# A GFNet-and-MLP kernel: the first transforms take turns over four PSUM banks, and one split store at the end changes its queue

## The chip, the cores and the metric

The kernel runs on one core of a Trainium2 chip. The metric is the time of one execution in microseconds (us), the median over several runs. Five engines work side by side: PE (TensorE, matrix products), DVE (VectorE), ACT (ScalarE), POOL (GpSimd) and SP (SyncE, which here only issues DMAs). PE writes its results to PSUM banks; DVE or ACT must copy a bank out before PE may fill it again.

## The reference, cut to what matters

```python
def _attn_ref(x, filt_r, filt_i):              # x: (8, 3008, 256)
    X = np.fft.rfft(x, axis=1)
    F = (filt_r + 1j * filt_i)[None, :, :]     # (1505, 256)
    y = np.fft.irfft(X * F, n=x.shape[1], axis=1)
    return y.astype(np.float32)

def _moe_ref(x, w_in, w_out):                  # x: (24064, 256), d_ff = 2048
    h = x @ w_in
    g = np.maximum(0.01 * h, h)
    return (g @ w_out).astype(np.float32)
```

The result is `_moe_ref` of the filtered sequence: a Fourier transform along 3008 tokens, a product with a filter, the inverse transform, and two matrix layers with a leaky ReLU between them.

## The kernel before, in words

**Transforms.** 3008 is factored as 94 x 32. A batch's transform has four stages, each a row of small matmuls into one PSUM bank that ACT or DVE copies out: `s1_group` (L254, copied at L257), `s2_group` (L303, multiplied by the filter on DVE at L309 to L315 and added on POOL at L318), `sa_group` (L325, L327) and `sb_group` (L346, copied into `yt` at L336). Between stages the data is turned through DRAM by DMAs that SP issues. The first batch takes a way of its own, without DRAM, written out by hand in the list `FIRST`; its last six groups are called later, by `late_sb` (L446, matmuls at L437).

**The two layers.** The 24064 tokens form 47 chunks of 512. `moe1` (L495) makes the first layer: for each pair of 128-column blocks four matmuls (L505) into a double bank `ph`, of which there are two in turn, and one leaky ReLU on ACT (L510) from `ph` into `gt`. One chunk later the second layer follows: `plain` (L626, matmuls at L630) for the first three chunks, then `products`, a Strassen-Winograd form of it with seven half-size products (L561 to L624, matmuls at L569), whose sums are made on DVE (L542, L594, L602 and others).

**Banks.** PSUM's eight banks are the two double banks `ph0` and `ph1`, three single banks `pf0` to `pf2`, and `po_ps`. The opening uses the first seven, and `po_ps` for matmuls on zeros (`keep_warm`). Then `single.pop()` (L489) takes `pf2` out of the list from which `bank("pf", ...)` (L154) deals to the transforms in turn; `pf2` (as `psp_last`) and `po_ps` become `out_banks`, the second layer's. So from there on the transforms alternate between `pf0` and `pf1`.

**Order.** Every step is a function put at a planned time with `at(time, f)` in a heap; at the end the heap is emptied in order of time, and each function issues its instructions, on whichever engine, in that order. A planned time is in units in which a chunk lasts `SL = 8`: `moe1` of chunk 0 has times 0 to 7.5, and the second layer of chunk 0 begins at 8.01. The transforms' groups of batches 1 to 7 are placed by `plan` and the loop after it (L688 to L706), at least `GAP = 0.6` units apart. Engines run their queues strictly in this order, so an instruction that waits holds up those behind it on its engine.

**Stores.** A chunk's output leaves in four stores of 128 tokens, `tj = 2 * i + j`, two from each of the tiles `rows(ci, 0)` (h0) and `rows(ci, 1)` (h1). Output tokens lie in groups of `QT = 376`, so a store that meets such a border becomes two DMAs (the loop in `store`, L548). In the last chunk, number 46, one border falls 8 tokens into store `tj = 1` (i = 0, j = 1), which is then one DMA of 8 tokens (2 x 4 rows of 256) and one of 120 (30 x 4 rows). For chunk 46 the stores with j = 1 are issued by ACT, those with j = 0 by SP; for all other chunks all are issued by SP. h1 is stored when its last DVE sum (L602) is done, h0 when the very last sum of the kernel (L594) is done.

Of the kernel before, what the change touches and what calls it, by code (L numbers as in the profile page):

```python
# [75 lines left out]
def kernel(  # L76
# [9 lines left out]
    nc = tc.nc  # L86
# [7 lines left out]
    NCHUNK = TOK // CH  # L94
    assert NCHUNK * CH == TOK
    SL = 8
# [52 lines left out]
    single = [psp.tile([P, CH], FP32, name=f"pf{i}") for i in range(3)]  # L149
    po_ps = psp.tile([P, 2, D], FP32, name="po_ps")  # L150
    psp_last = single[-1]
# [12 lines left out]
    def at(time, f):  # L164
        clock["n"] += 1
        heapq.heappush(work, (time, clock["n"], f))
# [315 lines left out]
    for step in FIRST.split(","):  # L482
# [7 lines left out]
    out_banks = [t[:].rearrange("p (a t d) -> p a t d", a=2, t=2)  # L490
                 for t in (psp_last, po_ps.rearrange("p a d -> p (a d)"))]

    gts, osts, phs = {}, {}, {}

    def moe1(ci, ct):  # L495
# [52 lines left out]
    def store(ci, tj, of, queue=nc.sync):  # L548

        t, end = ci * CH + tj * P, ci * CH + (tj + 1) * P  # L550
        lo = 0
        while t < end:
            e = min(end, (t // QT + 1) * QT)
            b, h = divmod(t // QT, N2 // 4)
            row = b * N + (t % QT) // 4 * N2 + 4 * h
            queue.dma_start(
                bass.AP(tensor=out.tensor, offset=out.offset + row * D,
                        ap=[[N2 * D, (e - t) // 4], [D, 4], [1, D]]), of[lo : lo + e - t])
            lo, t = lo + e - t, e
# [15 lines left out]
    def rows(ci, i):  # L575

        if (ci, i) not in osts:
            osts[ci, i] = outp.tile([P, 2, 3, P], FP32, tag="ost", name=f"ost_c{ci}_h{i}")
        return osts[ci, i]

    def stores(ci, i, of=range(2)):
        for j in of:
            store(ci, 2 * i + j, rows(ci, i)[:, j, 0:2, :].rearrange("p k d -> p (k d)"),
                  nc.scalar if ci == NCHUNK - 1 and j else nc.sync)

    def twice(po):
        ap = [list(v) for v in po.ap]
# [4 lines left out]
    def last_product(ci):  # L592
        def after(po):
            add(rows(ci, 0)[:, :, 1], po, rows(ci, 1)[:, :, 2], AL.add)  # L594
            soon(AFTER[5], lambda: stores(ci, 0))
        return product(ci, lambda: sum_places(ci)[3], b22, after, 3)

    def products(ci):
        a11, a12, a21, a22 = (lambda i=i, j=j: quarter(ci, i, j) for i in range(2) for j in range(2))

        def after5(po):
            add(rows(ci, 1)[:, :, 1:3], twice(po), part[1], AL.add)  # L602
            soon(AFTER[5], lambda: stores(ci, 1))

        def m1():
            return product(ci, a11, b11, lambda po: nc.scalar.copy(t1, po))

        def m2():
            return product(ci, a12, b21, lambda po: add(rows(ci, 0)[:, :, 0], po, t1, AL.add))

        def m7():
            return product(ci, lambda: sum_places(ci)[1], wt[2], lambda po: add(v7, po, t1, AL.add), 1)

        if ci == NCHUNK - 1:
            items = last_product(ci - 1) + m1() + m7() + m2()
        elif ci > W0:
            items = m1() + last_product(ci - 1) + m2() + m7()
        else:
            done["products"] += 1
            items = m1() + [lambda: None] * (2 * NCH) + m2() + m7()  # L620
        items += product(ci, lambda: sum_places(ci)[2], wt[1], lambda po: add(part[1], twice(po), part[0], AL.add), 2)
        items += product(ci, a22, wt[3], lambda po: add(rows(ci, 1)[:, :, 0], po, u3, AL.add))
        items += product(ci, lambda: sum_places(ci)[0], wt[0], after5, 0)
        return items + last_product(ci) if ci == NCHUNK - 1 else items  # L624
# [44 lines left out]
    for b in range(1, B):  # L669
        z = 47 * (b - 4) if b > 4 else 0  # L670
        p = PLANS[min(b, 4) - 1]
# [82 lines left out]
```

## Time and profile before

| What | Value |
|---|---|
| median of 6 runs | 749.81 us (749.54 to 752.38) |
| the profiled execution's own time | 751.97 us |
| its span, first to last instruction | 750.2 us |
| PE busy | 738.1 us (98%) |
| ACT busy | 559.2 us (75%) |
| DVE busy | 501.4 us (67%) |
| POOL busy | 169.5 us (23%) |
| granted TensorE clock | 0.999 |
| last matmul begins, last sum on DVE begins | 744.2, 744.51 us |

The span is counted from the first instruction; 1.8 us of the execution lie around it. PE's busy time counts pipelined matmuls with modelled ends, so a PE that is busy is not thereby at its fastest; how fast it goes is read from the distance between the starts of its matmuls. The first batch's opening ends at about 35 us, the chunks of the two layers with the transforms between them fill the time to about 744 us, and the last 6 us hold only the stores and the closing barrier.

### The profile page before, as it was taken

The numbers are of one execution on the slowest core, as the hardware profiler recorded it, in microseconds if no ns is written. First come the engines' busy times: TensorE is split into PE (matmuls) and PEld (weight loads), VectorE is DVE, ScalarE is ACT, GpSimd is POOL, SyncE is SP. The second block draws the span as 40 slices with busy tenths as digits, with TensorE's granted clock in tenths as the row PEclk, the third lists the DMA queues.
The fourth block names the chain that finished last, engine by engine and source line by source line (L and its number), as shares of the span: only waits on it lengthen the run. The fifth ranks groups of instructions, "written<-read, shape, count | busy, mean of one in ns | idle before, by whom it ended". The sixth has DMA issues, their size and how long they took to land.

```text
span 750.2 us, 19408 instructions
## 1 busy us (share of the span) xinstructions
PE 738.1 (98%) x8017; PEld 528.8 (70%) x8017; DVE 501.4 (67%) x684; ACT 559.2 (75%) x755; POOL 169.5 (23%) x171
## 2 busy tenths in 40 slices
PE   8999999999999999999999999999999999999996
PEld 3656667677677777877778777777777777777775
DVE  5986646776666776766667757766676676565565
ACT  3776797888778778787787787787777777777662
POOL 5603421432232212221232232121212210000000
PEclk9999999999999999999999999999999999999999
DMA  9997798887866567655675656544454333111011
GB/s 206 227 222 187 187 219 222 208 202 194 203 181 168 143 192 184 153 140 163 197 177 156 158 152 173 157 138 112 142 161 120 100 107 107 50 54 54 32 53 59
DMA packets 119560, 113.64 MB, mean 151 GB/s; under 512 B 16352, under 2 KB 92768, under 8 KB 119280
## 3 DMA queue, kind: packets, MB, share of 16 engines
q1 hardware_dynamic: 104127, 94.66, 42.5%
q0 software_dynamic: 15056, 17.49, 15.8%
q8 instruction: 62, 1.02, 0.6%
q10 hardware_dynamic: 289, 0.26, 0.1%
q14 instruction: 26, 0.21, 0.1%
HBM read 57.51 MB, written 50.33 MB: 144 GB/s over the span
## 4 chain that ended last, share of the span: by engine, by line
PE 94%; DVE 2%; DMA 2%; ACT 1%; POOL 0%; issue 0%; SPq 0%; DVEq 0%; POOLq 0%
PE ph L505 43%; PE po_ps L569 18%; PE pf L569 18%; PE pf L254 3%; PE pf L346 3%; PE pf L325 2%; PE pf L303 2%; PE pf L630 1%; PE po_ps L630 1%; DMA p_b_g<-p_b_g 1%; DMA big<-in_x_dram 1%; PE po_ps L368 1%; POOL y_b_g L318 0%; ACT yt L336 0%; PE ph L396 0%
## 5 line engine op out<-in xcount | busy, mean ns | idle before, releaser
L510 ACT ACTIVATE gt_c<-ph 128x1024 f16<-128x1024 f32 x376 | 385.3, 1025 | 134.9 <-PE ph L505 124.2
L505 PE MATMUL ph<-yt,w_in_sb 128*128 128x512 f16 (+7 forms) x1728 | 447.3, 351 | 0.2 <-ACT yt L336 0.2
L569 PEld LDWEIGHTS <-gt_c 128*128 128x128 f16 x2800 | 202.3, 98 | 91.3 <-issue 0.2
L318 POOL TENSOR_TENSOR y_b_g<-p_b_g,p_b_g 128x512 f16<-128x512 f32 x84 | 119.8, 1427 | 414.3 <-DMA p_b_g<-p_b_g 241.3
L569 PEld LDWEIGHTS <-big 128*128 128x128 f16 x2128 | 151.3, 98 | 62.9 <-issue 1.4
L505 PEld LDWEIGHTS <-w_in_sb 128*128 128x128 f16 x1728 | 137.4, 98 | 20.3 <-issue 0.7
L312 DVE TENSOR_TENSOR p_b_g<-pf,fb_sb 128x512 f32<-128x512 f32 x78 | 53.7, 688 | 32.4 <-PE pf L303 17.1
L569 PE MATMUL po_ps<-wt_sb,gt_c 128*128 128x128 f16 x704 | 70.0, 219 | 0.0
L569 PE MATMUL pf<-wt_sb,gt_c 128*128 128x128 f16 x688 | 68.4, 219 | 0.0
L569 PE MATMUL pf<-w_out_sb,gt_c 128*128 128x128 f16 x720 | 67.9, 219 | 0.0
L569 PE MATMUL po_ps<-wt_sb,big 128*128 128x128 f16 x720 | 67.4, 219 | 0.1
L569 PE MATMUL pf<-wt_sb,big 128*128 128x128 f16 x704 | 67.2, 219 | 0.0
L257 ACT CAST big<-pf 128x512 f16<-128x512 f32 x100 | 58.3, 588 | 11.9 <-PE pf L254 10.5
L569 PE MATMUL po_ps<-w_out_sb,gt_c 128*128 128x128 f16 x688 | 66.0, 219 | 0.0
L336 ACT CAST yt<-pf 128x376 f16<-128x376 f32 x120 | 56.4, 473 | 10.8 <-PE pf L346 7.7
L542 DVE TENSOR_TENSOR big<-gt_c 128x2048 f16<-128x2048 f16 (+1 forms) x46 | 57.4, 1248 | 0.1
L315 DVE TENSOR_TENSOR p_b_g<-pf,fa_sb 128x512 f32<-128x512 f32 x84 | 57.2, 681 | 0.2
L542 DVE TENSOR_TENSOR gt_c<-gt_c 128x2048 f16<-128x2048 f16 x43 | 55.5, 1290 | 1.0
L542 DVE TENSOR_TENSOR big<-big,gt_c 128x2048 f16<-128x2048 f16 (+1 forms) x45 | 55.6, 1236 | 0.1
L542 DVE TENSOR_TENSOR big<-gt_c,big 128x2048 f16<-128x2048 f16 (+1 forms) x45 | 54.5, 1211 | 0.0
L327 ACT CAST big<-pf 128x512 f16<-128x512 f32 x84 | 49.0, 584 | 6.1 <-PE pf L325 4.2
L254 PE MATMUL pf<-x_sb,small_sb 94*128 94x512 f16 x112 | 42.7, 381 | 0.6 <-ACT big L257 0.6
(88 smaller groups left out, 620.3 us busy)
## 6 DMA issues: line engine op xcount, KB each, us to landing
dz<-big SPq DMA_DIRECT2D x98, 256.0 KB
p_b_g<-p_b_g SPq DMA_DIRECT2D x156, 128.0 KB
out_dram<-ost_c_h SPq DMA_DIRECT2D x119, 128.0 KB
big<-dz SPq DMA_DIRECT2D x42, 256.0 KB
big<-dz SPq DMA_DIRECT2D x56, 192.0 KB
x_sb<-in_x_dram POOLq DMA_DIRECT2D x40, 192.0 KB, 4.3
x_sb<-in_x_dram POOLq DMA_DIRECT2D x2, 768.0 KB, 8.4
w_in_sb<-in_moe_w_in_dram POOLq DMA_DIRECT2D x1, 1024.0 KB, 12.5
```

Source lines behind the costliest of these rows:

```text
L254: nc.tensor.matmul(ps, fwd1[:N1], x_sb[:N1, ds(2 * g, 2), :], start=True, stop=True)
L257: copy(st[:, ds(2 * (g % 2), 2), :], ps)
L312: nc.vector.tensor_tensor(p2[:], ps, fb, AL.mult)
L315: nc.vector.tensor_tensor(p1[:], ps, fa, AL.mult)
L318: ("y", b, g), lambda: nc.gpsimd.tensor_tensor(y1[:], p1[:], p3[:], AL.add)))
L327: nc.scalar.copy(st2[h % 4][:, ds(2 * (g % 2), 2), :], ps)
L336: copy(yv, ps.rearrange("p c a -> p a c"))
L346: nc.tensor.matmul(ps[:, j, :], z2[h % 4][:K4, j, ts(dt, P)], i1_sb[:K4, 4 * h + j, :], start=True, stop=True)
L505: nc.tensor.matmul(ph[:, j, ds(t - ci * CH, e - t)], w_in_sb[:, dt, ts(ct, P)], yt[:, dt, ds(t % N, e - t)], start=(dt == 0), stop=(dt == ...
L510: nc.scalar.activation(gts[ci][:, ds(2 * g, 2), :], ph, AF.Lrelu)
L542: nc.vector.tensor_tensor(*(v[:, ds(c0, n)] for v in (o, i0, i1)), op)
L569: nc.tensor.matmul(po[:, t], a()[:, c, ts(t, P)], w[:, c, :], start=(c == 0), stop=(c == NCH - 1))
```

## The change

Two edits.

The first puts `pf2` and `po_ps` back into the list from which the transforms' banks are dealt, and takes them out again at planned time 7.6, shortly before the second layer's first matmul. In that stretch the transforms take turns over four banks, not two. Fourteen groups fall into it: thirteen of `s1_group` of batch 1 and one `late_sb`. The counter of turns runs on, and fourteen is even, so every group after it gets the bank that it had before.

The second changes the queue of two of the last chunk's four stores: ACT issues those with i = j (h0 j 0 and h1 j 1), SP those with i != j. The store that the border splits (h0 j 1, two DMAs) goes from ACT to SP, and h0 j 0 (one DMA) from SP to ACT.

```diff
     out_banks = [t[:].rearrange("p (a t d) -> p a t d", a=2, t=2)
                  for t in (psp_last, po_ps.rearrange("p a d -> p (a d)"))]
 
+
+    single += [psp_last, po_ps.rearrange("p a d -> p (a d)")]
+    at(SL - 0.4, lambda: single.__delitem__(slice(2, 4)))
+
     gts, osts, phs = {}, {}, {}
...
     def stores(ci, i, of=range(2)):
         for j in of:
             store(ci, 2 * i + j, rows(ci, i)[:, j, 0:2, :].rearrange("p k d -> p (k d)"),
-                  nc.scalar if ci == NCHUNK - 1 and j else nc.sync)
+                  nc.scalar if ci == NCHUNK - 1 and i == j else nc.sync)
```

The lines after the first edit stand four lines lower in the changed kernel.

## The prediction

> **What bounds the kernel now.** I read the page's busy rows first, then PE's waits, then the two places that the diff touches: the stretch of planned times 0 to 7.6, and the end.
>
> ```profile
> PE 738.1 (98%) x8017; PEld 528.8 (70%) x8017; DVE 501.4 (67%) x684; ACT 559.2 (75%) x755; POOL 169.5 (23%) x171
> ```
>
> PE is busy in 98% of the span, and its granted clock (0.999 on average) leaves nothing to win. Time can come only from PE's gaps, or from what lies after its last matmul. The longest waits of PE after its very first one, in the whole trace (line, what it waited for: total us, times, longest):
>
> ```profile
> PE ph L374 <- ACT x_sb L459: 1.1, 1, 1.1
> PE pf L325 <- POOL y_b_g L318: 1.1, 1, 1.1
> PE pf L303 <- DVE p_b_g L315: 1.0, 1, 1.0
> PE pf L254 <- ACT big L257: 0.6, 1, 0.6
> ```
>
> Only the last row can belong to the first edit: one matmul of an s1 group waited until ACT had copied an earlier group out of the same bank. Its place, in PE's timeline (start, us, instruction, idle before) and ACT's:
>
> ```profile
> 41.06 0.38 PE L254 MATMUL pf<-x_sb,small_sb 94*128 94x512 f16 x1
> 41.27 0.59 PE L505 MATMUL ph<-yt,w_in_sb 128*128 128x512 f16 x2
> 41.80 0.45 PE L437 MATMUL pf<-i_sb,big 128*64 128x94 f16 x8
> 42.81 0.38 PE L254 MATMUL pf<-x_sb,small_sb 94*128 94x512 f16 x1 [0.56 <-ACT big L257]
> ```
>
> ```profile
> 41.26 1.02 ACT L510 ACTIVATE gt_c<-ph 128x1024 f16<-128x1024 f32 x1 [0.36 <-PE ph L505]
> 42.17 0.58 ACT L257 CAST big<-pf 128x512 f16<-128x512 f32 x1
> 42.64 0.49 ACT L336 CAST yt<-pf 128x376 f16<-128x376 f32 x1
> 43.65 2.11 ACT L510 ACTIVATE gt_c<-ph 128x1024 f16<-128x1024 f32 x2 [0.52 <-PE ph L505]
> ```
>
> The group of 41.06 is copied out only at 42.17 to 42.75, behind a leaky ReLU on ACT. The second group after it (42.81) has the same bank, and PE, in order, stands still. Elsewhere in this stretch PE goes on without a gap: an s1 matmul and two of the first layer start every 0.65 us, three of 512 columns at 0.22 each.
>
> The end, from the timeline of the two issuing queues, and SP's waits:
>
> ```profile
> 744.33 0.54 SPq L556 DMA_DIRECT2D out_dram<-ost_c_h  x1
> 744.97 0.55 SPq L556 DMA_DIRECT2D out_dram<-ost_c_h  x1
> ...
> 744.34 0.68 ACTq L556 DMA_DIRECT2D out_dram<-ost_c_h  x1
> 745.11 1.21 ACTq L556 DMA_DIRECT2D out_dram<-ost_c_h  x1
> 746.37 0.93 ACTq L556 DMA_DIRECT2D out_dram<-ost_c_h  x1
> ...
> SPq L749 <- DMA out_dram<-ost_c_h: 3.3, 3, 1.7
> ```
>
> SP has issued its two stores by 745.52. ACT needs until 747.30: its first, then the piece of 8 tokens (1.21), then the piece of 120 (0.93). SP's longest last wait, 1.7 us, is for that piece to land, at about 749.0; the closing barrier takes the rest to 750.2. So the end is set by ACT's queue.
>
> **The change part by part.** *Four banks.* The instructions and their order on PE, DVE, ACT and POOL stay as they were but for bank names and waits; nothing is added. The group of 42.81 gets a bank whose copy (on DVE) was over by 41.51, so it may start when PE gets there. The same switch from L437 to a full-width matmul at 48.00 took 0.37 us start to start (48.00 to 48.37); so 41.80 + 0.37 = 42.17 in place of 42.81: 0.63 us.
>
> What is late next? ACT's next leaky ReLU began at 43.65, 0.42 after the last first-layer matmul that it needs. With PE 0.63 earlier these are ready at 43.02, and ACT is free of its two copies at 43.13: it starts at about 43.05 and ends at 44.07. PE writes that `ph` bank again with the first-layer matmul now at 44.76, then at 44.13. Margin 0.06. I take no new stall; at worst a tenth or two comes back. A new wait for the other `ph` bank stands at 42.81 (was 43.45), and the ReLU that frees it ended at 42.28.
>
> The borrowed banks are the second layer's. Its first matmul (L630, `po_ps`, 46.49, then 45.86) gets a wait for DVE to have copied the last s1 group out of `po_ps`; that group's matmul is the one at 44.54, copied by about 45.6, then 0.6 earlier: 0.8 before it is needed. Behind that wait all of PE would queue. Its wait for the weights `w_out_sb` moves to the weight load; their DMA was issued at 29.2 and took 14.1, so they are there at 43.3. `pf2` is wanted at 51.1, long after. On DVE the copies follow PE; L664, filling 41.43 to 42.37, is done before the earlier group is ready at 42.58. If that cover failed, DVE's 0.95 would put the copy behind, not PE.
>
> Does 0.63 reach the end? From 46 us on the turning stores, loads, exchanges and copies all start from PE's results and SP's order, so they shift with PE. The DMA engines are busy near fully from 37 to 52 us, and the last s1 store is issued at 51.74, when this is nearly over; the loads at 56.67 wait in SP's queue for the store of the second output (DVE L635 at 55.47), PE's work again. PE's later stalls (1.0 at 66, 1.1 at 213) hang on DVE and on POOL, whose inputs shift likewise. I carry 0.63.
>
> *The split store.* SP now issues h1 j 0 (744.33 to 744.87), the 8-token piece, the 120-token piece; ACT h1 j 1 and h0 j 0. On SP the same two shapes stand in this trace at 261.90 and 408.47:
>
> ```profile
> 261.90 0.73 SPq L556 DMA_DIRECT2D out_dram<-ost_c_h  x1
> ...
> 408.47 0.93 SPq L556 DMA_DIRECT2D out_dram<-ost_c_h  x1
> ```
>
> By these rows: 744.97 + 0.73 + 0.05 + 0.93 = 746.68 against 747.30: 0.62 us gained. ACT's h0 j 0, 745.11 + 0.6 to 0.7, is done by 745.8 and lands before.
>
> [...] the 8-token piece took 1.21 on ACT beside SP's 0.55, 0.48 above its 0.73 on SP alone; yet ACT's first store, begun with SP's, took 0.68 and not 0.54 + 0.54. [...] Between 0.1 and 0.62 I take 0.45: [...] of the two contended rows one shows 0.14 lost and one 0.48.
>
> *Sum.* 0.63 + 0.45 = 1.08. The profiled execution, 751.97 with its span of 750.2, would be 750.9 with a span of 749.1. It stood 2.2 above the median of the runs; off that median, 749.81, the sum gives 748.7.
>
> **Rivals.** *PE's stall moves to ACT.* ACT follows so closely that the 0.06 margin fails, and the leaky ReLU is PE's next wait. For it: ACT goes 43.65 to 45.76 without a pause. Against: in the stretch it still has idle time, 0.52 before 43.65. If it takes 0.4 of the 0.63[...]: 749.81 - 0.23 - 0.1 = 749.5, no measurable change.
>
> *A later wait goes as well.* PE's two long later stalls, 1.0 on DVE at 66 us and 1.1 on POOL at 213 us, end when a chain of DVE work, exchange DMA and POOL add ends. The exchanges make POOL wait 241 us in all, 11.7 at the longest, so their length varies with what they meet. If the shift lets one such chain through, 0.5 to 1.1 is added: 749.81 - 1.08 - 0.7 = 748.0. Against: each shifts with PE, so only chance meetings decide.
>
> *Slower: the exchange comes late.* The same chain in the other direction, at L325 in batches 1 to 7: PE asks for `y` 0.63 earlier, while the exchange meets other traffic and does not come earlier. One such slip exists and costs 1.1. With three more, 3.3 - 1.08: 752.0. It decides from about 2.6 us of new waits on. Against: the exchange is issued from DVE products that follow PE.
>
> **How the numbers follow.** 0.2% of 749.81 is 1.5 us, about what a measurement of this kernel can tell from no change; five of the six runs lie within 749.5 to 750.4. Both parts as summed (0.7 to 1.3): 0.60; the gain of 1.1 is only 0.4 from the bound, and with that scatter a quarter of it, 0.15, reads as over 1.5. A later wait goes as well: 0.28. Stall moved to ACT: 0.05. Late exchange: 0.07. Faster 0.15 + 0.28 = 0.43, same 0.45 + 0.05 = 0.50, slower 0.07. The range, 747.9 to 749.7, holds the sum with both ends of the tail (748.6 and 749.1), most of the case with a later wait, and scatter at both ends; the late exchange and the extremes are left out.
>
> **What would show it.** In the changed profile: PE's wait at L254 for ACT is gone and the s1 matmul after the first L437 row starts 0.37 after it; the second layer's first matmul comes about 0.63 earlier, the last matmul too; SP's last issue ends about 1.8 after its 8-token piece began, with ACT done before. Wrong would be: a new wait of PE on ACT L510 near 44 us, a larger wait at L325, or SP's last issue ending no earlier, counted from the last sum, than ACT's did, 2.4 after it.

## The result, and the profile after

The changed kernel takes 748.94 us in the median (748.11 to 750.21, 20 runs), beside 750.10 for the kernel before in the same runs (41). The ratio is 0.9982, 95% interval 0.9976 to 0.9988: 1.2 us by the medians, 1.35 by the ratio (0.0018 x 750.1); the interval runs from 0.9 to 1.8 us, so the gain is clear of noise. The forecast was 748.7, 1.1 below the median that it started from.

PE's waits after the change (the whole table of that view):

```profile
PE po_ps L368 <- DVE one L226: 1.2, 1, 1.2
PE pf L303 <- DVE p_b_g L315: 1.0, 1, 1.0
PE ph L392 <- issue: 0.5, 1, 0.5
PE ph L420 <- POOL prod L400: 0.4, 1, 0.4
PE ph L437 <- DVE big L429: 0.2, 1, 0.2
PE ph L374 <- ACT x_sb L459: 0.2, 1, 0.2
```

The row of L254 waiting for ACT is gone. So is the row of L325 waiting for POOL, 1.1 us, which no part of the change aimed at; more on it below. PE's timeline at the place of the old wait:

```profile
40.62 0.38 PE L254 MATMUL po_ps<-x_sb,small_sb 94*128 94x512 f16 x1
40.84 0.59 PE L509 MATMUL ph<-yt,w_in_sb 128*128 128x512 f16 x2
41.36 0.45 PE L437 MATMUL pf<-i_sb,big 128*64 128x94 f16 x8
41.74 0.39 PE L254 MATMUL pf<-x_sb,small_sb 94*128 94x512 f16 x1
...
43.70 0.38 PE L509 MATMUL ph<-yt,w_in_sb 128*128 128x512 f16 x1
```

and ACT's beside it:

```profile
41.74 0.58 ACT L257 CAST big<-po_ps 128x512 f16<-128x512 f32 x1
42.20 0.49 ACT L336 CAST yt<-pf 128x376 f16<-128x376 f32 x1
42.60 2.11 ACT L514 ACTIVATE gt_c<-ph 128x1024 f16<-128x1024 f32 x2
```

The group of 40.62 now writes `po_ps`. ACT copies it as late as before, at 41.74, but the group that starts at the same 41.74 has another bank and does not wait: 0.38 us from L437's start to L254's, before 1.01 (41.80 to 42.81). ACT's next leaky ReLU starts at 42.60 without a pause; the first of its pair ends at about 43.62, and PE fills that `ph` bank again at 43.70. PE did not catch up with it.

The end, on SP and then on ACT:

```profile
741.82 0.54 SPq L560 DMA_DIRECT2D out_dram<-ost_c_h  x1
...
742.45 0.70 SPq L560 DMA_DIRECT2D out_dram<-ost_c_h  x1
...
743.20 0.90 SPq L560 DMA_DIRECT2D out_dram<-ost_c_h  x1
```

```profile
741.82 0.67 ACTq L560 DMA_DIRECT2D out_dram<-ost_c_h  x1
...
742.59 0.70 ACTq L560 DMA_DIRECT2D out_dram<-ost_c_h  x1
```

The last sum on DVE starts at 741.99. SP's pieces of 8 and 120 tokens take 0.70 and 0.90; its last issue ends at 744.10, 2.1 after that start. Before, ACT's ended at 747.30, 2.8 after 744.51. So the last issue ends 0.7 earlier, counted from the sum.

**Where the profiled 3.3 us went.** The two profiled spans, 750.2 and 746.9, differ by more than the medians do. Three marks of each timeline split the difference: the first matmul of the first layer (L505, now L509), the first of the second layer (L630, now L634), and the start of the last sum on DVE (L594, now L598).

| stretch | before | after | difference |
|---|---|---|---|
| start to first layer | 34.96 | 34.46 | -0.50 |
| first layer to second layer | 11.53 | 10.98 | -0.55 |
| second layer to last sum | 698.02 | 696.55 | -1.47 |
| last sum to end of span | 5.65 | 4.95 | -0.70 |

Only the second and the fourth row contain what was changed, 1.25 us together. The first and the third vary from one execution to the next, as the experiments show.

### The profile page after: what moved, and what is told of

Read it like the earlier page. It is cut to its first block, busy times and chain, and to the rows that moved or that the text cites. A ratio compares the mean times of both kernels' runs of the same rounds, so it can differ in the third digit from the quotient of the medians.

```text
span 746.9 us, 19408 instructions
## 1 busy us (share of the span) xinstructions
PE 737.9 (99%) x8017; PEld 528.7 (71%) x8017; DVE 503.6 (67%) x684; ACT 559.2 (75%) x755; POOL 167.0 (22%) x171
## 4 chain that ended last, share of the span: by engine, by line
PE 91%; DMA 5%; DVE 1%; POOL 1%; ACT 1%; SPq 1%; issue 0%; POOLq 0%; DVEq 0%
PE ph L509 42%; PE po_ps L573 18%; PE pf L573 18%; PE pf L254 3%; PE pf L346 3%; PE pf L325 2%; PE pf L303 2%; PE pf L634 1%; PE po_ps L634 1%; DMA f_sb<-fwd_const 1%; DMA fa_sb<-in_filt_i_dram 1%; DMA out_dram<-ost_c_h 1%; DMA dz<-big 1%; POOL prod L400 0%; DVE big L546 0%
## 5 line engine op out<-in xcount | busy, mean ns | idle before, releaser
L509 PE MATMUL ph<-yt,w_in_sb 128*128 128x512 f16 (+7 forms) x1728 | 447.3, 351 | 0.2
L318 POOL TENSOR_TENSOR y_b_g<-p_b_g,p_b_g 128x512 f16<-128x512 f32 x84 | 117.2, 1397 | 415.1 <-DMA p_b_g<-p_b_g 240.0
L509 PEld LDWEIGHTS <-w_in_sb 128*128 128x128 f16 x1728 | 137.5, 98 | 19.7 <-DVE yt L336 0.4
L546 DVE TENSOR_TENSOR gt_c<-gt_c 128x2048 f16<-128x2048 f16 x43 | 57.8, 1345 | 1.0
L254 PE MATMUL pf<-x_sb,small_sb 94*128 94x512 f16 x109 | 41.6, 381 | 0.0
```

Source lines behind the costliest of these rows:

```text
L254: nc.tensor.matmul(ps, fwd1[:N1], x_sb[:N1, ds(2 * g, 2), :], start=True, stop=True)
L318: ("y", b, g), lambda: nc.gpsimd.tensor_tensor(y1[:], p1[:], p3[:], AL.add)))
L509: nc.tensor.matmul(ph[:, j, ds(t - ci * CH, e - t)], w_in_sb[:, dt, ts(ct, P)], yt[:, dt, ds(t % N, e - t)], start=(dt == 0), stop=(dt == ...
L546: nc.vector.tensor_tensor(*(v[:, ds(c0, n)] for v in (o, i0, i1)), op)
```

## The experiments

The theory: the change takes away one wait of PE (0.6 us) and shortens the issuing of the last stores (0.5 to 0.7); these add, and nothing else changed. Rivals: PE's earlier start removes the wait at L325 as well; the issues of SP and ACT lengthen each other, as ACT's row of 1.21 us beside SP's 0.55 suggested, and that eats up the gain at the end; the two edits need each other.

**The banks alone.** The changed kernel with the stores of before:

```diff
-                  nc.scalar if ci == NCHUNK - 1 and i == j else nc.sync)
+                  nc.scalar if ci == NCHUNK - 1 and j else nc.sync)
```

> The four banks alone, stores as before. Theory: PE's wait of 0.6 us at L254 is gone and nothing else changes, so the median falls by 0.6 us (0.5 to 0.7) and PE's stream from 46 us on runs 0.6 earlier; the tail from the last DVE sum's start to the end stays at 5.65 us. Rival (the wait of PE at L325 for POOL near 213 us goes because PE runs earlier): the fall is 1.9 us, in every run. Rival (the two edits need each other): no fall.

Measured: 749.55 against 750.13, ratio 0.9995 (0.9986 to 1.0003). The medians say -0.58, what was expected, though the interval alone cannot tell it from nothing. The profile can: the wait is gone, the stretch from the first to the second layer is 10.92 us and not 11.53, and the tail is 5.6. A fall of 1.9 lies outside the interval (its far end is 1.05): the wait at L325 is not part of the edit's effect.

**The stores alone.** The kernel before with the diff's second edit only.

> The queue swap alone, banks as before. Theory: PE's stream is that of before, with the 0.6 us wait at L254; the tail from the last DVE sum's start to the end falls from 5.65 to 4.9 us, and the median by 0.7 us (0.6 to 0.8). Rival [...]: the tail falls by 0.1 to 0.3 only. Rival (the gain is all in PE's part): no fall.

Measured: 749.57 against 750.13, ratio 0.9992 (0.9984 to 1.0001), -0.56 by the medians; again the interval alone does not exclude no change. Of its PE waits, the one in question:

```profile
PE pf L254 <- ACT big L257: 0.6, 1, 0.6
```

The wait at L254 is back, the stretch from the first to the second layer is 11.53 again, and the tail is 4.95, not the rival's 5.35 to 5.55. In the profiles each edit does its own part without the other, so neither needs the other. The medians fit a plain sum (0.58 and 0.56 alone, 1.16 together), but with such intervals that is weak support. The wait at L325 is missing here too, with two banks in turn.

**Three banks.** Only `pf2` is lent, stores as before:

```diff
-    single += [psp_last, po_ps.rearrange("p a d -> p (a d)")]
-    at(SL - 0.4, lambda: single.__delitem__(slice(2, 4)))
+    single += [psp_last]
+    at(SL - 0.4, lambda: single.__delitem__(slice(2, 3)))
```

> Three banks in the early stretch in place of four (pf2 added, po_ps not), stores as before. Theory: one more bank is enough, since the group that waited then takes the bank of the third group before it, which DVE had emptied 1.2 us earlier; the same fall as with four banks, 0.6 us (0.5 to 0.7). Rival (four are needed, since copies on DVE run late too): a wait of PE at L254 stays, and the fall is under 0.3 us.

Measured: 749.53 against 750.13, ratio 0.9991 (0.9983 to 0.9999). PE's timeline:

```profile
41.01 0.45 PE L437 MATMUL pf<-i_sb,big 128*64 128x94 f16 x8
41.39 0.39 PE L254 MATMUL pf<-x_sb,small_sb 94*128 94x512 f16 x1
```

The same 0.38 from start to start, and the stretch is 10.92. One more bank was enough; the fourth took nothing more off this stretch.

**The pieces apart.** Four banks, and the split store's two pieces on two queues:

```diff
-            queue.dma_start(
+            (queue[lo > 0] if isinstance(queue, tuple) else queue).dma_start(
...
-                  nc.scalar if ci == NCHUNK - 1 and i == j else nc.sync)
+                  (nc.sync, nc.scalar) if ci == NCHUNK - 1 and (i, j) == (0, 1)
+                  else nc.scalar if ci == NCHUNK - 1 and i and j else nc.sync)
```

> Four banks, and the two pieces of the split store on two queues: SP issues h1 j 0, h0 j 0 and the 8-token piece, ACT issues h1 j 1 and the 120-token piece. Theory (issue times simply add on each queue): SP ends 0.55 + 0.05 + 0.70 = 1.3 us after it may begin, ACT 0.1 + 0.95; the last issue ends 0.3 to 0.35 us earlier than in the changed kernel, whose SP needs 1.65, and the median is 0.3 us below it, 1.6 below before. Rival [...]: the three issues add up to about 2.2 us whatever the queue, no gain over the changed kernel or a loss of up to 0.5.

Measured: 748.54 against 750.13, ratio 0.9979 (0.9971 to 0.9986); tail 4.57. On ACT:

```profile
742.82 0.69 ACTq L560 DMA_DIRECT2D out_dram<-ost_c_h  x1
...
743.62 1.44 ACTq L560 DMA_DIRECT2D out_dram<-ost_c_h  x1
```

The piece of 120 tokens took 1.44 us on ACT, where it had taken 0.93 as ACT's last DMA before and 0.90 on SP after. Neither expectation has that number: not the plain sum, and not issues in turn, which ACT's 0.70 beside SP's 0.70 in the changed kernel (742.59 to 743.29 and 742.45 to 743.15) contradicts. ACT's last issue thus ended 2.06 us after the last sum's start, hardly earlier than SP's 2.11 in the changed kernel, and yet the tail is 0.38 shorter; the reason comes further down. What ACT's slow pieces have in common, here and in the kernel before, is another thing: each was the first DMA of ACT that was not of the full 32 x 4 shape.

**All of h0 on ACT.** The kernel before with SP silent beside ACT's pieces:

```diff
-                  nc.scalar if ci == NCHUNK - 1 and j else nc.sync)
+                  nc.scalar if ci == NCHUNK - 1 and (j or i == 0) else nc.sync)
```

> Banks as before; all of h0's last stores on ACT (h1 j 1, h0 j 0, the 8-token piece, the 120-token piece), SP issues only h1 j 0. No SP issue lies beside ACT's pieces. Theory A (the 8-token piece took 1.21 us on ACT because SP was issuing beside it[...]): it now takes 0.73. Theory B (ACT is slow the first time that it issues a DMA whose outer count is not a multiple of 16): it takes about 1.2 again and the 120-token piece behind it 0.93. Either way the last issue ends later than before.

Measured (one run, 750.55 us, of which only the profile is read), ACT's last three issues of four:

```profile
743.00 0.69 ACTq L556 DMA_DIRECT2D out_dram<-ost_c_h  x1
743.73 1.21 ACTq L556 DMA_DIRECT2D out_dram<-ost_c_h  x1
744.99 0.95 ACTq L556 DMA_DIRECT2D out_dram<-ost_c_h  x1
```

With nothing beside it, the 8-token piece takes 1.21 again. Theory A (contention with SP) falls; theory B (the first of its kind on ACT) stands, though its bound at multiples of 16 was not shown: no run put a 16 x 4 store on ACT. A full store takes ACT 0.69 here with SP silent, as long as beside SP. The tail grew to 6.4 us.

**A first DMA of that kind earlier.** Two kernels made from the pieces apart. In one, which ran once (748.85 us), ACT also issues the split store of chunk 43:

```diff
-                  else nc.scalar if ci == NCHUNK - 1 and i and j else nc.sync)
+                  else nc.scalar if (ci == NCHUNK - 1 and i and j) or (ci, i, j) == (43, 0, 1) else nc.sync)
```

> The kernel of e4_pieces_apart, plus: the split store of chunk 43 (two DMAs, 40 and 88 tokens) issued by ACT and not SP, some 40 us before the end; it holds ACT up there, so only the tail is to be read. Theory B, with or without forgetting over 700 us: ACT's first of those two is slow (1.2 or more), the second about 0.85, and the 120-token piece at the end takes 0.93. Theory A: it takes 1.44 at the end.

```profile
713.27 1.40 ACTq L560 DMA_DIRECT2D out_dram<-ost_c_h  x1
...
714.72 0.84 ACTq L560 DMA_DIRECT2D out_dram<-ost_c_h  x1
...
743.00 0.89 ACTq L560 DMA_DIRECT2D out_dram<-ost_c_h  x1
```

The first, of 40 tokens, is now the slow one; the one at the end takes 0.89, beside SP's issues as in the pieces apart. The tail is 4.60, no shorter than the pieces apart have it. In the other, ACT issues a DMA of 2 rows of 8 bytes in the opening:

```diff
     nc.scalar.activation(one[:], one[:], AF.Lrelu)
+    warm_q = cpool.tile([2, 4], FP16, name="warm_q")
+    nc.scalar.dma_start(warm_q[:], small_d.ap()[0:2, 0, 0:4])
```

> The kernel of e4_pieces_apart, plus one tiny DMA (2 rows of 8 bytes) that ACT issues in its idle opening, before the first x has landed; the rest is the same. Theory B (first issue of that kind on ACT is slow[...]): ACT's 120-token piece at the end takes 0.93 us and not 1.44, the last issue ends about 0.3 us earlier than in e4, and the median is 0.3 below e4's, 1.9 below before. Theory A [...]: the piece still takes 1.44, no change to e4. Theory B with forgetting [...]: as A.

```profile
742.49 0.97 ACTq L562 DMA_DIRECT2D out_dram<-ost_c_h  x1
```

0.97 in place of 1.44, after 741 us in between. But the tail only fell from 4.57 to 4.50, where I had expected 0.3. The DMA engines tell more. A row of this view begins with its window in us and ends with their busy share and their GB/s; between stand the five engines' busy times, all zero by then, and the clock. First the pieces apart, then the kernel with the early DMA:

```profile
744.00:745.20 1.20, 0.00 (x0) 0.00 (x0) 0.00 (x0) 0.00 (x0) 0.00 (x0) 1.00 0.92 324
745.20:746.00 0.80, 0.00 (x0) 0.00 (x0) 0.00 (x0) 0.00 (x0) 0.00 (x0) 1.00 0.63 170
...
742.90:744.10 1.20, 0.00 (x0) 0.00 (x0) 0.00 (x0) 0.00 (x0) 0.00 (x0) 1.00 0.95 324
744.10:744.80 0.70, 0.00 (x0) 0.00 (x0) 0.00 (x0) 0.00 (x0) 0.00 (x0) 1.00 0.70 192
```

Counted from the last sum's start, the engines move the last stores from 1.0 to 3.0 us in the one and from 1.0 to 2.9 in the other, without a pause, though ACT's last issue ends at 2.06 in the one and at 1.59 in the other. (In the changed kernel they end at 3.4: there the 120-token piece is SP's third issue, and begins only at 1.20.) ACT's own packets end between 2.9 and 3.0 in every profile of the pieces apart, with a row of 1.44, 0.97 or 0.89. So the long row did not hold up its own transfer, and ACT's issuing no longer set this end. Whether the transfers did, or SP's third issue, which ends at 1.76 in all of them, no run here separates. In the kernel before it was otherwise. There the 120-token piece had to wait on ACT's queue behind the long row, and the DMA engines stood still for a whole microsecond (the end of that piece's issue is 747.30):

```profile
746.90:747.90 1.00, 0.00 (x0) 0.00 (x0) 0.00 (x0) 0.00 (x0) 0.00 (x0) 1.00 0.00 0
```

The median of the kernel with the early DMA, 747.97 against 750.32, ratio 0.9964 (0.9952 to 0.9976), fell by more than the tail explains; only six runs stand behind it.

**Once more, together.** The changed kernel and the two best, on one chip.

> The changed kernel, unchanged, beside the next two on one chip. Expected 1.2 to 1.4 us below before (0.61 from the banks, 0.71 from the stores); tail from the last sum's start to the end 4.95 us.

> The kernel of e4_pieces_apart again. Its tail was 4.57 us, so 0.38 below the changed kernel if the tail is all that differs.

> The kernel of e9_act_split_early again. Its tail was 4.50 us: ACT's piece had become 0.46 us faster, but SP, whose three issues end 1.76 us after the sum's start in both, then set the end. If the tail is all that differs, it lies 0.07 us below e11, no difference that can be measured; if the extra DMA of the opening shortens the opening, it lies 0.3 us or more below.

| kernel | median | before | ratio (95%) | tail |
|---|---|---|---|---|
| changed kernel | 748.73 | 750.28 | 0.9980 (0.9972 to 0.9988) | 4.94 |
| pieces apart | 748.75 | 750.28 | 0.9980 (0.9974 to 0.9987) | 4.53 |
| pieces apart, early DMA on ACT | 748.38 | 750.28 | 0.9977 (0.9968 to 0.9987) | 4.50 |

The changed kernel's 1.55 by the medians is above the 1.2 to 1.4 expected. The shorter tail of the pieces apart shows in every profile, but its 0.4 us does not show in these medians, nor is the early DMA's 0.37 clear of the intervals. All three beat the kernel before; which of them is best stays open. Whether the early DMA does something to the opening was not settled: its two profiles have the first layer begin at 34.11 and 34.09, those of the pieces apart at 35.55 and 34.31.

**The kernel before, profiled again.**

> The kernel before, unchanged, for a second profile. Theory (the 1.3 us stall of PE at L325 near 213 us is a chance meeting of transfers and no property of this kernel): it is absent or of another size; the 0.6 us wait at L254 near 42 us and the tail of 5.65 us are there again. Rival (it belongs to the two-bank order): it is there again with 1.0 to 1.3.

From its PE waits:

```profile
PE ph L374 <- ACT x_sb L459: 1.9, 1, 1.9
...
PE pf L254 <- ACT big L257: 0.6, 1, 0.6
```

The wait at L254 and the tail of 5.65 are there again; the wait of 1.1 at L325 is not, nor is it in the two other profiles with two banks in turn. The opening's wait for x, 1.1 in the first profile, is 1.9. Over the thirteen profiles of this study the first layer begins anywhere from 33.85 to 35.55 us, and the stretch from the second layer to the last sum lasts 696.5 to 698.0, under both bank orders: the changed kernel's own second profile has 697.8. So the first and third row of the table above are scatter, and the two rows that the edits touch explain 1.25 us, with which the 1.35 of the ratio agrees.

## Why the prediction was right

*The bound.* PE sets the pace (busy in 98% of the span before, 99% after), and time came only from one gap of PE and from behind its last matmul, as argued.

*Four banks: 0.63.* The stretch is 11.53 in all four profiles with two banks in turn, 10.92 in eight of the nine with more, and 10.98 in the changed kernel's first: 0.61, and 0.58 by the medians. No new stall: the margin to ACT's ReLU, put at 0.06, was about 0.08. That the gain reached the end rests on the medians and on the long stretch behind, which was no longer with the banks lent (696.5 to 697.8) than without (696.7 to 698.0).

*The split store: 0.45.* The direction was right and this term was sized too small: 0.70 in the profiles (5.65 to 4.95). The rows of the trace, 0.73 and 0.93, gave 0.62; the rest lies in SP's pieces, which took 0.70 and 0.90. The 0.17 that I had cut off was an estimate for queues that issue in turn, and the weak step. Its lower end, a gain of 0.1, puts SP's 0.73, ACT's 0.55 and SP's 0.93 one behind the other from 744.97 on, to 747.2, which is 2.7 after the sum's start; the changed kernel took 2.1, with SP's and ACT's issues side by side at 0.70 and 0.70. Both rows that I took for contended had another cause. The 1.21 on ACT came again with SP silent, and so did the length of a full store: ACT takes 0.69 for it alone, so its 0.68 beside SP's 0.54 had lost nothing. Full stores took ACT 0.64 to 0.70 in these profiles; a loss smaller than that scatter is not excluded.

*The sum.* 1.08 was forecast; 1.16 and 1.55 were measured by the medians of two sets of runs, 1.35 by the first ratio. With the 0.70 the sum would have been 1.3. So the gain lies close to the 0.2% bound of 1.5, inside it in the first set and just over it in the second, and that the likeliest case came true was in part luck.

*The rivals.* The stall did not move to ACT. "A later wait goes as well" looked true in the first pair of profiles, where the 1.1 at L325 is gone; it was chance, since it is missing from the kernel before's second profile too, and from the other two with two banks. The late exchange did not come.

## What to carry to other kernels

A pair of profiles tells more than their difference: split both at marks around the edits, and take a second profile before a vanished wait is credited to the change. Where banks are dealt in turn, look for the latest copy in the turn; here one bank borrowed from a stage that had not begun took away the one wait of that stretch, 0.56 us. At the end of a kernel, count the time that each queue needs to issue the last stores, piece by piece. A long row costs what it holds up: here the issue behind it on its queue, in the kernel before (a row of 1.21 us, and later 1.0 us in which the DMA engines stood still), and next to nothing when it was the queue's last and the DMA engines were busy anyway (1.44 against 0.97, the tail 4.57 against 4.50).

## What the runs showed of the hardware

ACT's first DMA with an outer count (the number of groups of 4 rows, for these stores) of 2, 10 or 30 had a row about half a microsecond longer than such rows otherwise have; no run had ACT begin with another count below 32. For 30 x 4 rows it was 1.44 us, in the pieces apart, against 0.89 to 0.97 when one of 2 or 10 had gone before, even one of 16 bytes 741 us earlier. It was 1.21 for 2 x 4 (in the kernel before, and with all of h0 on ACT) and 1.40 for 10 x 4; no later row of these shapes on ACT was recorded, but on SP, in the kernel before, they took 0.71 to 0.73 and 0.79 to 0.85. Full 32 x 4 stores that ACT had issued ahead, two of 0.69 us with all of h0 on ACT, did not help. The extra time held up the next issue on ACT's queue (the 120-token piece of the kernel before, issued from 746.37 on), not the transfer of its own DMA: ACT's packets ended 2.9 to 3.0 us after the last sum's start with a row of 1.44 as with one of 0.97 or 0.89. What makes the first one long was not shown.

The length of a row went by the outer count and did not follow the bytes. Of SP's stores in the kernel before, the median row was 0.59 us for 32 x 4 and for 16 x 4 rows, 0.70 to 0.74 for 2, 4 and 8 x 4, and 0.80 to 0.93 for the other counts, all even, from 6 to 30. So a store cut into 8 and 120 tokens cost SP 0.73 + 0.93 in place of 0.59.
